# Window attention and two expert layers on one core: the places of the weights in SBUF, and of the identity

## The chip, the cores and the metric

The kernel runs on one core of one Trainium2 chip, in one launch. The metric is device time in microseconds (us), from the run's own clock; the trace comes from a further execution with the hardware profiler on. Engines are called by their short names in the rows: PE is TensorE (PEld its weight loads), DVE VectorE, ACT ScalarE, POOL GpSimd, and SP the engine that issues the DMAs.

## The reference

Three stages follow each other, all in float32. B = 2, H = 8, S = 768, D = 64.

```python
# 1. attention over a window of +-15 keys and the maxima of 24 blocks of 32 keys
k_sum = k.reshape(B, H, nb, block, D).max(axis=3)
v_sum = v.reshape(B, H, nb, block, D).mean(axis=3)
scores_l = scale * q @ k.T            # masked to |i - j| < 16
scores_s = scale * q @ k_sum.T + log(32)
a = softmax(concat([scores_l, scores_s]))
x = a @ concat([v, v_sum])            # -> (1536, 512)
# 2. first layer, 512 -> 2048 -> 512
h = x @ w_in;  g = max(h, 0) + alpha * min(h, 0);  x = g @ w_out
# 3. second layer, with a rational function of h
h = x @ w_in2
g = (a0 + a1*h + a2*h**2 + a3*h**3) / (1 + |b0|*|h| + |b1|*h**2 + 1e-6)
out = g @ w_out2
```

The weights of both layers reach the kernel as 64-bit words, eight bytes for a number, and the kernel makes its own number pairs of them.

## The kernel before

**Numbers in two parts.** Each operand of the layers' matmuls is split into a high part (`xh`, `gh`, `wih`, `woh`) and a low part (`xl`, `gl`, `wil`, `wol`). A product of two operands is three matmuls: high with high, and high with low both ways. All are in the float32r type, with 128 columns loaded and 512 streamed, or 256 in the first part of the first layer.

**Layers.** The 1536 tokens go in three units of 512, the 2048 hidden columns in 16 steps f of 128. `h_mm` (L186) makes h of one unit and one f with 4 x 3 = 12 matmuls on line L195; `y_mm` (L244) adds g's share to the four output tiles with 12 matmuls on line L258. In h of both layers, and in y of the first layer, a weight is the loaded operand (lhsT) and x or g is streamed. In y of the second layer it is the other way round: g is loaded, and the weight `woh` or `wol` is streamed. From about 150 us on, TensorE does a run of 12 for h, then a run of 12 for y, of a step that is some steps behind, and so on. In the second layer h of the last step comes well before the end, so the last 48 matmuls are y alone.

**Weights.** `w_load` (L143) fetches 1 MB of weight words into one of two raw tiles, from the second byte on, with one DMA from the SP queue. `w_split` (L150) turns it into a high and a low tile in steps: ScalarE makes `top` (L161), VectorE joins it with the raw words to `cv` (L163), ScalarE copies cv rounded into the high tile (L137, a helper's line), and GpSimd subtracts the two for the low tile (L173). There are 16 high and 16 low tiles of 4096 bytes in each partition, and they are filled twice, once for each layer. The last ones (`wih7` among them) lie where the attention's buffers lay before, and wait for those to be done with.

**Attention.** It is worked in 24 slices of 64 queries, until about 150 us, with the first layer's first steps between them. TensorE makes scores s (L392), the probabilities p are turned by a transpose against the 128 x 128 identity `ident` (L448), and multiplied with the values (L462). GpSimd multiplies p by the reciprocal of its sum (L442). The order of all this is written out by hand in tables (`ORDERS`, `ENG` and others), which the change leaves as they are.

**Places.** Every tile lies at one byte offset in all 128 partitions. Pools are laid one behind the other from the left (constants, x, g, temporaries, raw, cv, weights), and some, the attention's among them, from the right. SBUF is filled to the end: the last weight tile ends 128 bytes before it. The table gives the offset of some tiles as a remainder modulo 128, as the built program has them.

| tiles | before | after |
|---|---|---|
| `xh`, `xl`, `gh`, `gl`, and the temporaries | 64 | 64 |
| raw, two tiles in turn | 64 and 96 | 64 and 64 |
| `cv` | 0 | 64 |
| all weight tiles | 0 | 64 |
| `ident` | 0 | 64 |
| `qz`, `kc`, `vt`, `p`, `pT` of the attention | 64 | 64 |

The matmuls read offsets of whole multiples of 128 bytes within x, g and weight tiles, so the remainders hold for each matmul's operands.

Of the kernel before, what the change touches and what calls it, by code (L numbers as in the profile page):

```python
# [9 lines left out]
F32 = mybir.dt.float32  # L10
# [3 lines left out]
I16 = mybir.dt.int16  # L14
# [7 lines left out]
P = 128  # L22
# [48 lines left out]
def kernel(  # L71
# [14 lines left out]
    nc = tc.nc  # L86
# [14 lines left out]
    const = ctx.enter_context(tc.tile_pool(name="const", bufs=1))  # L101
# [3 lines left out]
    rawp = ctx.enter_context(tc.tile_pool(name="rawp", bufs=2))  # L105
# [5 lines left out]

    nc.scalar.preload_act_table_set("natural_log_exp_and_others")

    ident = const.tile([P, P], F32, name="ident")
    make_identity(nc, ident)
    al = const.tile([P, NF], F32, name="al")
    na = const.tile([P, 4], F32, name="na")
    ab = const.tile([P, 2], F32, name="ab")
# [22 lines left out]
            e.tensor_scalar(out=out, in0=in_, scalar1=scale, scalar2=None, op0=ALU.mult)  # L141

    def w_load(layer, nm, j):  # L143
        raw = rawp.tile([P, 4100], I16, tag="raw", name="raw")
        words = src_of[layer, nm][:, 2 * j:2 * j + 2, :].rearrange("p a b -> p (a b)").bitcast(I16)
        nc.sync.dma_start(out=raw[:, 1:4097], in_=words)
        raws[layer, nm, j] = raw
        loaded[layer, nm, j] = now[0]

    def w_split(layer, nm, j):  # L150

        raw = raws.pop((layer, nm, j))
        rest = raw.bitcast(I32)[:, 1:2049:2]
        w = cvp.tile([P, 1024], F32, tag="cv", name="cv")
        w3 = w.rearrange("p (a b) -> p a b", a=2)  # L160
        nc.scalar.activation(out=top.bitcast(F16)[:, 1::2], in_=raw.bitcast(BF16)[:, 4:4100:4], func=AF.Copy)  # L161
        yield "low"
        nc.vector.scalar_tensor_tensor(out=w.bitcast(I32), in0=rest, scalar=13, in1=top,  # L163
                                       op0=ALU.logical_shift_right, op1=ALU.bitwise_or)
        if loads:
            w_load(*loads.pop(0))
        yield "hi"
        hi = places[nm, j].tile([P, 2, 512], F32R, tag=f"{nm}h{j}", name=f"{nm}h{j}")
        lo = places[nm, j].tile([P, 2, 512], F32R, tag=f"{nm}l{j}", name=f"{nm}l{j}")
        copy("hi", hi, w3)  # L170
        for i, place in enumerate(("mid", "end")):
            yield place
            eng(place).tensor_tensor(out=lo[:, i, :], in0=w3[:, i, :], in1=hi[:, i, :].bitcast(F32), op=ALU.subtract)  # L173
        wts[layer, nm, j] = (hi, lo)
# [114 lines left out]
    a1 = att_p.enter_context(tc.tile_pool(name="a1", bufs=1, side="right"))  # L289
# [8 lines left out]
    att_e = ExitStack()  # L298
    e1 = att_e.enter_context(tc.tile_pool(name="e1", bufs=1, side="right"))

    NQZ, NVC, NVT = 3, 4, 4
    vlate = []
    HALF = S // 2 + 2 * WINDOW
# [262 lines left out]
    with tc.manual_schedule():  # L566
# [7 lines left out]
        for t in range(-1, LAST + 1):  # L574
# [33 lines left out]
            if t in WLOAD_AT:  # L608
                w_load(*loads.pop(0))
# [110 lines left out]
```

## Time and profile before

| | |
|---|---|
| time, median of 3 runs | 634.09 us (633.48 to 634.31) |
| the profiled execution | 632.7 us, of which the span 630.6 us |
| TensorE busy | 607.3 us, 96% of the span |
| ScalarE, GpSimd, VectorE busy | 384.3, 353.8 and 339.9 us |
| TensorE's share of the chain that ended last | 87% |
| first layer without attention | about 150 to 369 us |
| second layer | about 369 us to the end |

The span is the time from the first to the last instruction in the trace; what the profiled execution took beyond it lies before and after. Matmuls are pipelined: the recorded length of one (around 395 ns for 512 columns) is longer than the time to the next one's start, so the pace of TensorE is read from the runs in the chain of waits, where 12 matmuls of one line stand as one piece with the time that they took together.

### The profile page before, as it was taken

Reading aid. Unit: us, or ns where it says so; the run is one execution under the profiler, and the core shown is the slowest. Engines: PE = TensorE matmul, PEld = TensorE weight load, DVE = VectorE, ACT = ScalarE, POOL = GpSimd, SP = SyncE. Lnnn points to the kernel's source line nnn. Section 1 sums busy time; section 2 is a strip of 40 time slices with the busy share of each in tenths; the row PEclk is TensorE's granted clock in tenths of the full one; section 3 lists DMA queues with packets and bytes.
Section 4 is the critical chain, followed back from the end, with each engine's and each line's share of the span. In section 5 each row is a group of like instructions: output and inputs, shape, how many; then the busy total and the mean of one; then the engine's idle time right before and its main releaser. Section 6 shows DMA issues by size and latency. Waiting matters only on the chain.

```text
span 630.6 us, 8589 instructions
## 1 busy us (share of the span) xinstructions
PE 607.3 (96%) x3192; PEld 496.0 (79%) x3192; DVE 339.9 (54%) x494; ACT 384.3 (61%) x665; POOL 353.8 (56%) x343
## 2 busy tenths in 40 slices
PE   5689999999999999999999999999999999999997
PEld 2467989987888888888888888888888888888885
DVE  4756677753221111045555277776566666566664
ACT  1779798877343333367777457776466666466663
POOL 3266779666512222237667457886366666466662
PEclk9869999999999999999999999999999999999999
DMA  8997476525100000025545101000000000100001
GB/s 294 314 312 266 161 239 221 190 80 200 68 1 1 1 0 1 0 75 192 188 172 183 58 1 67 1 0 2 36 32 1 0 1 1 68 0 2 0 2 67
DMA packets 17129, 55.09 MB, mean 87 GB/s; under 512 B 2368, under 2 KB 4416, under 8 KB 12992
## 3 DMA queue, kind: packets, MB, share of 16 engines
q1 hardware_dynamic: 17088, 54.55, 25.0%
q8 instruction: 25, 0.41, 0.3%
q14 instruction: 16, 0.13, 0.1%
HBM read 51.39 MB, written 3.15 MB: 86 GB/s over the span
## 4 chain that ended last, share of the span: by engine, by line
PE 87%; ACT 4%; DMA 3%; DVE 2%; POOL 2%; issue 1%; SPq 1%; ACTq 0%; DVEq 0%
PE y L258 41%; PE h L195 41%; PE s L392 1%; PE pt L448 1%; PE po L462 1%; DMA raw<-in_w_in 1%; PE vps L357 1%; DMA na<-in_pa 1%; ACT top L161 1%; DMA kt<-in_kT 1%; POOL p L413 1%; ACT p L422 1%; DVE cv L163 1%; SPq L336 0%; ACT pT L137 0%
## 5 line engine op out<-in xcount | busy, mean ns | idle before, releaser
L195 PE MATMUL h<-xh,wih 128*128 128x512 f32 (+1 forms) x416 | 158.0, 380 | 0.0
L195 PE MATMUL h<-xl,wih 128*128 128x512 f32 (+1 forms) x416 | 157.3, 378 | 0.1
L195 PE MATMUL h<-xh,wil 128*128 128x512 f32 (+1 forms) x416 | 157.1, 378 | 0.0
L242 POOL TENSOR_TENSOR gl<-tp,gh 128x512 fp32r<-128x512 f32 (+1 forms) x75 | 94.3, 1258 | 85.8 <-ACT gh L137 84.4
L137 ACT ACTIVATE gh<-tp 128x512 fp32r<-128x512 f32 (+1 forms) x76 | 46.2, 608 | 94.6 <-PE y L258 50.7
L195 PEld LDWEIGHTS h<-xl,wih 128*128 128x128 f32 x416 | 78.4, 188 | 16.5 <-issue 0.5
L195 PEld LDWEIGHTS h<-xh,wih 128*128 128x128 f32 x416 | 78.4, 189 | 16.4 <-ACT pT L137 0.5
L195 PEld LDWEIGHTS h<-xh,wil 128*128 128x128 f32 x416 | 78.3, 188 | 16.0
L258 PE MATMUL y<-gh,woh 128*128 128x512 f32 (+1 forms) x224 | 82.9, 370 | 0.0
L258 PE MATMUL y<-gl,woh 128*128 128x512 f32 (+1 forms) x224 | 81.2, 362 | 0.0
L258 PE MATMUL y<-gh,wol 128*128 128x512 f32 (+1 forms) x224 | 81.2, 362 | 0.0
L163 DVE SCALAR_TENSOR_TENSOR cv<-raw,top 128x1024 int32<-128x1024 int32 x32 | 59.8, 1870 | 30.5 <-ACT top L161 23.1
L258 PE MATMUL y<-woh,gh 128*128 128x512 f32 x192 | 75.9, 395 | 0.0
L258 PE MATMUL y<-wol,gh 128*128 128x512 f32 x192 | 75.8, 395 | 0.0
L258 PE MATMUL y<-woh,gl 128*128 128x512 f32 x192 | 75.3, 393 | 0.0
L228 DVE SCALAR_TENSOR_TENSOR tu<-tu,h 128x512 f32<-128x512 f32 x48 | 33.0, 687 | 71.4 <-ACT h L227 62.8
L217 POOL TENSOR_SCALAR tu<-tv,ab 128x512 f32<-128x512 f32 x48 | 37.3, 777 | 61.0 <-ACT tv L215 61.0
L218 POOL TENSOR_TENSOR tu<-tu,tv 128x512 f32<-128x512 f32 x48 | 62.4, 1299 | 4.0
L242 POOL TENSOR_TENSOR gl<-tu,gh 128x512 fp32r<-128x512 f32 (+1 forms) x28 | 32.4, 1157 | 52.6 <-ACT gh L137 52.6
L208 DVE SCALAR_TENSOR_TENSOR tp<-h,tp 128x512 f32<-128x512 f32 (+1 forms) x28 | 17.2, 614 | 72.2 <-ACT tp L137 72.2
L226 ACT ACTIVATE h<-tu,lnb 128x512 f32<-128x512 f32 x48 | 33.2, 691 | 31.3 <-DVE tp L220 28.9
L208 DVE SCALAR_TENSOR_TENSOR tu<-h,tu 128x512 f32<-128x512 f32 (+1 forms) x28 | 17.2, 613 | 64.7 <-ACT tu L137 64.7
(79 smaller groups left out, 1063.3 us busy)
## 6 DMA issues: line engine op xcount, KB each, us to landing
raw<-in_w_in SPq DMA_DIRECT2D x16, 1024.0 KB, 4.6
raw<-in_w_out SPq DMA_DIRECT2D x16, 1024.0 KB, 4.6
qz<-in_qT SPq DMA_DIRECT2D x25, 256.0 KB, 5.1
vc<-in_vS SPq DMA_DIRECT2D x24, 192.0 KB, 5.1
kt<-in_kT SPq DMA_DIRECT2D x16, 208.0 KB, 5.2
vt<-in_vS SPq DMA_DIRECT2D x12, 256.0 KB, 4.9
out<-stage SPq DMA_DIRECT2D x12, 256.0 KB, 2.1
al<-in_alpha SPq DMA_DIRECT2D x1, 8.0 KB, 6.5
```

The lines of the kernel that those rows point to most:

```text
L137: e.activation(out=out, in_=in_, func=AF.Copy, scale=1.0 if scale is None else scale)
L161: nc.scalar.activation(out=top.bitcast(F16)[:, 1::2], in_=raw.bitcast(BF16)[:, 4:4100:4], func=AF.Copy)
L163: nc.vector.scalar_tensor_tensor(out=w.bitcast(I32), in0=rest, scalar=13, in1=top, op0=ALU.logical_shift_right, op1=ALU.bitwise_or)
L195: nc.tensor.matmul(out=ps, lhsT=a, rhs=b, start=(c == 0 and m == 0), stop=(c == NC - 1 and m == 2))
L208: nc.vector.scalar_tensor_tensor(out=t, in0=ps, scalar=0.0, in1=t, op0=ALU.max, op1=ALU.subtract)
L217: nc.gpsimd.tensor_scalar(out=q, in0=v, scalar1=ab[:, 1:2], scalar2=ab[:, 0:1], op0=ALU.mult, op1=ALU.add)
L218: nc.gpsimd.tensor_tensor(out=q, in0=q, in1=v, op=ALU.mult)
L226: nc.scalar.activation(out=A, in_=q, func=AF.Ln, scale=2.0 ** -LN_SHIFT, bias=lnb)
L228: nc.vector.scalar_tensor_tensor(out=q, in0=q, scalar=one, in1=A, op0=ALU.add, op1=ALU.mult)
L242: (eng("gl") if (u, f) != steps[-1] else nc.vector).tensor_tensor(out=gl, in0=t, in1=gh.bitcast(F32), op=ALU.subtract)
L258: nc.tensor.matmul(out=yps[c][:, c0:c0 + n] if layer == 0 else yps[c], lhsT=a, rhs=b, start=(f == 0 and c0 == 0 and m == 0), stop=(f == NF ...
L357: nc.tensor.matmul(out=vmean[b][0:KEYS, :], lhsT=mean[:, z0:z0 + KEYS], rhs=vt[b, i], start=(i == 0), stop=(i == NV - 1))
```

## The change

The raw tile is made 4160 16-bit words wide where it had 4100, that is 8320 bytes for 8200. The DMA, the conversion and the words that they touch are the same. Two raw tiles of 8200 bytes, each rounded up to 32, end at a multiple of 128, and so everything behind them started there; two of 8320 end 64 bytes past one. To make room, the identity leaves the pool of constants on the left, where it took 512 bytes, and is made in the attention's pool on the right, which is given up after the attention.

```diff
-    ident = const.tile([P, P], F32, name="ident")
-    make_identity(nc, ident)
     al = const.tile([P, NF], F32, name="al")
...
     def w_load(layer, nm, j):
-        raw = rawp.tile([P, 4100], I16, tag="raw", name="raw")
+        raw = rawp.tile([P, 4160], I16, tag="raw", name="raw")
...
     e1 = att_e.enter_context(tc.tile_pool(name="e1", bufs=1, side="right"))
 
+    ident = a1.tile([P, P], F32, name="ident")
+    make_identity(nc, ident)
     NQZ, NVC, NVT = 3, 4, 4
```

The instructions of TensorE, VectorE, ScalarE and SP stand in the same order as before. Lines between L114 and L299 are two lower after the change. On GpSimd, at the start of the program, the identity's memset stood ahead of two small ones (`lnb` and `exb` are constants of the second layer, `bias` is the attention's mask):

```order
L716 UNCONDITIONAL_BRANCH
masks.py:197 MEMSET ident 128x128
L121 MEMSET lnb 128x1
L122 MEMSET exb 128x1
L309 MEMSET bias_130 128x120
masks.py:199 ISA
masks.py:199 AFFINE_SELECT ident<-ident 128x128
```

After the change, the same stretch of GpSimd's program reads:

```order
L716 UNCONDITIONAL_BRANCH
L119 MEMSET lnb 128x1
L120 MEMSET exb 128x1
masks.py:197 MEMSET ident 128x128
L309 MEMSET bias_130 128x120
masks.py:199 ISA
masks.py:199 AFFINE_SELECT ident<-ident 128x128
```

The memset went behind the two small ones, and the select that completes the identity kept its place.

The other difference is one wait. On ScalarE, near the end of the attention, the copy into the high tile `wih7` waited for VectorE's cv alone (semaphores in brackets, `top`, `tp` and `gh` belong to the conversion and to the first layer):

```order
L161 ACTIVATE top_95<-raw_1727 128x1024 [waits DMAHW5_49]
L204 ACTIVATE tp_1944<-h_1931 128x512 [waits PE_49]
L137 ACTIVATE wih7_2039<-cv_1913 128x1024 [waits DVE_49]
L137 ACTIVATE tp_1944<-tp_1944,al_88 128x512 [waits Activation_49]
L137 ACTIVATE gh_1947<-tu_1883 128x512 [waits Pool_49]
```

After the change, the same five instructions are:

```order
L159 ACTIVATE top_90<-raw_1727 128x1024 [waits DMAHW5_49]
L202 ACTIVATE tp_1944<-h_1931 128x512 [waits PE_49]
L135 ACTIVATE wih7_2039<-cv_1913 128x1024 [waits DVE_49,Pool_49]
L135 ACTIVATE tp_1944<-tp_1944,al_83 128x512 [waits Activation_49]
L135 ACTIVATE gh_1947<-tu_1883 128x512 [waits Pool_49]
```

The order is the same; `wih7` lies 320 bytes further left and now touches a second buffer of p, so its copy also waits for GpSimd's last product there (L442), for which the low tile `wil7` had waited before.

## Rows read from the trace of the kernel before

**Rows 1.** Page, busy us (share of the span) and instructions of each engine

```profile
PE 607.3 (96%) x3192; PEld 496.0 (79%) x3192; DVE 339.9 (54%) x494; ACT 384.3 (61%) x665; POOL 353.8 (56%) x343
```

**Rows 2.** Page, the chain that ended last: shares of the span by line

```profile
PE y L258 41%; PE h L195 41%; PE s L392 1%; PE pt L448 1%; PE po L462 1%; DMA raw<-in_w_in 1%; PE vps L357 1%; DMA na<-in_pa 1%; ACT top L161 1%; DMA kt<-in_kT 1%; POOL p L413 1%; ACT p L422 1%; DVE cv L163 1%; SPq L336 0%; ACT pT L137 0%
```

**Rows 3.** Chain in order of time: start us, us, what

```profile
201.67 2.80 PE y L258 x12
204.47 2.80 PE h L195 x12
...
442.19 2.79 PE y L258 x12
444.99 2.80 PE h L195 x12
447.79 2.76 PE y L258 x12
...
615.19 11.02 PE y L258 x48
```

**Rows 4.** Stretches: us, busy (x) of PE, PEld, DVE, ACT, POOL, clock, DMA share, GB/s

```profile
150.00:369.00 219.00, 219.00 (x940) 176.48 (x939) 70.34 (x72) 113.06 (x162) 96.45 (x75) 1.00 0.21 76
...
200.00:240.00 40.00, 40.00 (x173) 32.22 (x172) 4.84 (x7) 13.65 (x23) 9.87 (x8) 1.00 0.00 0
320.00:360.00 40.00, 40.00 (x173) 32.20 (x173) 16.95 (x13) 23.48 (x32) 26.39 (x21) 1.00 0.40 147
```

**Rows 5.** Identity: GpSimd's timeline (start us, us), and its readers (ns min/median/max, first start)

```profile
0.74 0.20 POOL masks.py:197 MEMSET ident<- 128x128 f32 x1 [0.29 <-POOLq L708]
...
1.18 0.29 POOL masks.py:199 TENSOR_SCALAR_AFFINE_SELECT ident<-ident 128x128 f32<-128x128 f32 x1
...
L448 PE MATMUL pt<-ident,p x96: 272/273/469, 17.7 to 141.8; 128*120 128x128 f32 x96
```

**Rows 6.** Timeline of GpSimd and ScalarE around the copy into wih7

```profile
138.29 1.00 POOL L442 TENSOR_TENSOR p<-p,d 128x480 f32<-128x480 f32 x1
139.23 1.30 POOL L242 TENSOR_TENSOR gl<-tu,gh 128x512 fp32r<-128x512 f32 x1
...
148.20 1.05 ACT L137 ACTIVATE wih<-cv 128x1024 fp32r<-128x1024 f32 x1
```

**Rows 7.** Raw and cv: instructions on them (ns min/median/max), two conversions in turn

```profile
L161 ACT ACTIVATE top<-raw x32: 1349/1380/1401, 24.1 to 412.0; 128x1024 f16<-128x1024 bf16 x32
L163 DVE SCALAR_TENSOR_TENSOR cv<-raw,top x32: 1216/1906/2346, 28.1 to 414.5; 128x1024 int32<-128x1024 int32 x32
...
L173 POOL TENSOR_TENSOR wil<-cv,wih x32: 1273/1295/1306, 34.6 to 388.8; 128x512 fp32r<-128x512 f32 x32
...
287.16 2.34 DVE L163 SCALAR_TENSOR_TENSOR cv<-raw,top 128x1024 int32<-128x1024 int32 x1 [1.54 <-ACT top L161]
...
292.75 2.35 DVE L163 SCALAR_TENSOR_TENSOR cv<-raw,top 128x1024 int32<-128x1024 int32 x1 [1.60 <-ACT top L161]
```

**Rows 8.** Single matmuls at the end of two h runs, 447.4 and 441.8 us (busy, mean ns)

```profile
L195 PE MATMUL h<-xl,wih 128*128 128x512 f32 x1 | 0.4, 398 | 0.0
L195 PE MATMUL h<-xh,wil 128*128 128x512 f32 x1 | 0.4, 392 | 0.0
...
L195 PE MATMUL h<-xh,wil 128*128 128x512 f32 x1 | 0.4, 397 | 0.0
L195 PE MATMUL h<-xl,wih 128*128 128x512 f32 x1 | 0.4, 394 | 0.0
```

**Rows 9.** Chain in order of time, runs of 256 columns in the first layer

```profile
106.38 1.42 PE y L258 x12
107.80 1.41 PE h L195 x12
...
112.69 1.36 PE h L195 x12
```

**Rows 10.** Two matmuls that follow each other in a first-layer h run, 205.3 us

```profile
L195 PE MATMUL h<-xh,wih 128*128 128x512 f32 x1 | 0.4, 393 | 0.0
```

## Prediction

> **What bounds the kernel now.** I read the page's busy times first. TensorE is busy for 96% of the span [rows 1], and from 150 us, where the attention ends, it never pauses: 219.00 of 219.00 us up to the second layer [rows 4]. The shares of the chain of waits say the same: two lines of TensorE, L195 (h) and L258 (y), are 41% of the span each [rows 2]. So next to nothing on another engine is worth a microsecond after 150 us. What counts there is how fast TensorE gets through one matmul after another.
>
> The chain in order of time gives that rate, since h and y stand in it as runs of 12 matmuls [rows 3]. A run of 512-column matmuls lasts 2.80 us in the first layer, for h and for y: 2.80 / 12 = 233.3 ns from one matmul to the next. The granted clock of that stretch is 1.00, the upper level of 2.4 GHz [rows 4], where 512 columns alone need 512 / 2.4 = 213.3 ns. So about 20 ns of each matmul are not its columns. Are they other engines' doing? Two stretches of 40 us, one with VectorE, ScalarE and GpSimd busy for 5, 14 and 10 us and no DMA, one with 17, 23 and 26 us and a DMA share of 0.40, hold 173 matmul records each [rows 4]. So the 20 ns belong to TensorE and its own operands.
>
> One thing in the chain does move that rate. In the second layer h still takes 2.80 us a run, but y alternates between 2.76 and 2.79 us, and the closing 48 matmuls of y, with no h between them, last 11.02 us, or 229.6 ns each [rows 3]. What differs in y there is the operands' roles. Everywhere else a weight (0 past a multiple of 128) is loaded and x or g (64 past) streams; there g is loaded and the weight streams. The change touches just these places, and gives both operands 64.
>
> **The change part by part.** *Identity.* Its memset, 0.20 us at 0.74 us, goes behind two that write one column each; the select that finishes it stays where it was, at 1.18 us, and the first transpose is at 17.7 us [rows 5]. Cost nothing: 16 us of cover. Were the cover gone, it would be the 0.2 us of the memset. As the streamed operand of 96 transposes it goes from 0 to 64; a transpose is recorded at 273 ns [rows 5], and if its pace moved by the 1.5% that y's does, 96 times 4 ns make 0.4 us, either way. I take 0.
>
> *The new wait.* ScalarE's copy into wih7 now waits for GpSimd's product on p. That product is over at 138.29 + 1.00 = 139.29 us, the copy starts at 148.20 us [rows 6]: 8.9 us of cover. If it were late, the product with alpha and the gh copy queue behind it on ScalarE, and y on TensorE waits for gh. I take 0.
>
> *Places under the other engines.* The conversion has its raw tile at 64 and at 96 by turns now, and writes cv at 0. ScalarE's part lasts 1349 to 1401 ns over all 32 [rows 7], so the two places differ by at most 0.05 us. VectorE's ranges from 1216 to 2346 ns, but two that follow each other, and so read different raw tiles, last 2.34 and 2.35 us; GpSimd's subtractions that read cv have a median of 1295 ns [rows 7], and one that reads tu and gh, all at 64, lasts 1.30 us at 139.23 us [rows 6]: no dearer. 32 conversions times 0.05 us are 1.6 us, of which only those on the chain before 150 us count: top is 1% of it and cv 1% [rows 2]. Bounds plus and minus 0.2 us; I take 0. The transfers keep their shapes and their start two bytes into the tile. The trace has no separate row for raw tiles at 96 and at 64; loads are 1% of the chain, some 6 us [rows 2], and if half of them, those into the second tile, moved by a tenth, it would be 0.3 us, either way. I take 0.
>
> *Operands of the matmuls.* This is the term that decides. 88 runs of h and 40 of y in the first layer are 512 columns wide, all with places 0 and 64; 48 runs of y in the second have the roles swapped; another 32 runs are 256 wide. No row shows 64 with 64 in a steady run. It stands only at the seams of the second layer, where the last h of a run streams x while the first g is loaded: one such matmul is recorded at 392 ns where its neighbour has 398, another at 397 beside 394 [rows 8]. One below, one above: undecided. So I bound it. From below: no stall at all, 213.3 ns or 2.56 us a run, saves 0.24 x 128 + 0.215 x 48 = 41 us. From above: the 256-wide runs show that the very same instructions at the same places take 1.36 or 1.41 to 1.42 us [rows 9], some 4%, according to how loads and streams fall together; 4% on 176 runs of 2.80 us is 20 us more. The rows nearest to the new state are y's of the second layer, where the loaded operand already lies at 64: (2.76 + 2.79) / 2 = 2.775 us. I take it for all 512-wide runs: 128 x 0.025 = 3.2 us saved, y of the second layer unchanged, the 256-wide runs 0, as they lie among waits on ScalarE and VectorE.
>
> The Trainium skill speaks against even this. "TensorE: Matmul & The Clock Gate", section "Step-by-step: what each phase is for", says that the loading of weights and the moving operand have read ports of their own and that a load takes nothing from the running matmul; by it, and with the 2.5 ns of its section "Back-to-back issue gap" as an estimate, a matmul would take 216 ns wherever its operands lie. The trace does not agree in size: 233.3 ns, and y's 229.6 at other places.
>
> *Sum.* The profiled execution took 632.7 us, with a span of 630.6 us and 2.1 us around it. 632.7 - 3.2 = 629.5 us. It lies 1.4 us under the median of the runs shown, 634.09, so for a median I add it back: 630.9 us.
>
> **The rivals.**
> *A large gain (chance 0.10).* Equal places bring loads and streams into the better of the two states of the 256-wide runs. 2.80 x 1.36 / 1.42 = 2.68 us: 0.12 x 128 + 0.095 x 48 = 19.9 us, so 614 us. For it: that state exists, and it lasts through whole runs [rows 9]. Against it: no 512-wide run of the first layer ever shows it, while 256-wide ones at one set of places show both.
>
> *Places don't matter (0.20).* y's 2.76 and 2.79 are then an effect of order, since the weight streams there in the sequence high, low, high. The time stays at 634.1 us. For it: even and odd runs of y differ by more (0.03 us) than the even ones differ from 2.80 [rows 3], though all have the same places modulo 128. The rule of the Trainium skill on separate ports, cited above from "TensorE: Matmul & The Clock Gate", would have it so as well.
>
> *The streamed operand's own place counts (0.10).* Weights stream well from 0 and lose that at 64, loaded operands don't matter. Then y of the second layer goes to 2.80 us: 44 x 0.025 + (4 x 2.80 - 11.02) = 1.1 + 0.2 = 1.3 us more, 635.4 us. For it: it explains why only this y is quicker. It sits on the line between no change and slower.
>
> *Equal places collide (0.18).* A load and a stream whose starts agree modulo 128 get in each other's way more often than two whose starts differ, and every matmul goes to the slower of the two recorded lengths that now alternate, 398 instead of the mean of 393 and 398 [rows 8, 10]. That is 2.5 ns x 12 = 0.03 us on each of 128 runs, 3.8 us, and y of the second layer goes with them, from 2.775 to 2.83 us, 2.6 us more: 640.5 us. It decides from the first 512-wide run on. The 397 at the seam speaks for it, the 392 against [rows 8].
>
> **How the numbers follow.** Forecast 0.42 (630.9 us), large gain 0.10, no change 0.20, streamed place 0.10, collision 0.18. A measurement of this kernel can tell about 0.2%, 1.27 us, from no change. Faster by more: 0.42 + 0.10 = 0.52. Within: 0.20 and four tenths of the streamed-place case, 0.24. Slower: the rest of that and the collision, 0.24. The range reaches down to 616 us, near the large gain, whose size is the least known of all, and up to 638.5 us, which takes in the streamed place with its small terms and a collision of about two thirds the size; outside lie about half of the one and half of the other rival. For the likeliest case alone it is 628 to 632.5 us, a mean run of 2.75 to 2.79 us.
>
> **What would show it right or wrong.** In the chain of the changed kernel, h and first-layer y should stand at about 2.775 us a run where 2.80 stood, with y of the second layer as it was; 2.68 would be the large gain, 2.80 with y at 2.80 the streamed place, 2.83 and more the collision, and the old numbers no influence. The matmul records in two 40 us stretches would go from 173 to 174 or 175. The identity is right if the first transpose still starts at about 17.7 us, the new wait if the wih7 copy starts within a few tenths of 148.2 us. I am wrong altogether if the time moves while the run lengths stay.

## The result and the profile after

The changed kernel takes 622.78 us (621.42 to 623.92, 4 runs) where the kernel before, on the same chip, takes 633.79 us (633.09 to 634.31): a ratio of 0.9826, with a 95% interval of 0.9803 to 0.9849. It is 11.0 us faster; 3.2 us were forecast. The two profiled executions, from which the rows are read, took 632.7 and 623.16 us and differ by 9.5 us.

The chain of the changed kernel in order of time, start us and us, at the places of [rows 3]. Lines between L114 and L299 are two lower now, so h is L193 and y is L256:

```profile
201.80 2.72 PE y L256 x12
204.52 2.72 PE h L193 x12
...
441.16 2.72 PE y L256 x12
443.88 2.72 PE h L193 x12
```

Once the attention is over, every run of 512 columns is 2.72 us, h and y, first layer and second, odd and even, up to the last steps: 226.7 ns a matmul for 233.3. The alternation of 2.76 and 2.79 is gone.

The runs of 256 columns in the attention, where [rows 9] had 1.42, 1.41 and 1.36:

```profile
107.84 1.44 PE y L256 x12
109.28 1.44 PE h L193 x12
...
112.80 1.43 PE y L256 x12
114.23 1.44 PE h L193 x12
...
129.10 2.75 PE h L193 x12
```

They are slower, and both states have become one. The first 512-wide runs, four of them between pieces of the attention, last 2.75 to 2.76 us and not yet 2.72. The first of h starts at 129.10 us; before, it stood in the same chain at 127.29 us. This start moves by more than that from one profiled execution to the next, as the later runs show, so only 0.02 to 0.08 us for each of 32 runs is surely the places' doing, 0.04 us on average.

Near the end a wait has appeared that the kernel before did not have. These are the last pieces of the chain:

```profile
612.09 0.76 DVE tp L228
...
612.93 0.64 ACT gh L135
...
613.61 3.07 PE y L256 x12
```

and this is its row among TensorE's waits (total us, times, longest us):

```profile
PE y L256 <- ACT gh L135: 1.1, 1, 1.1
```

The stretches with little and with much work on other engines, answering to [rows 4] (columns as there):

```profile
150.00:369.00 219.00, 219.00 (x967) 181.38 (x968) 73.75 (x77) 117.28 (x168) 102.21 (x78) 1.00 0.22 77
200.00:240.00 40.00, 40.00 (x178) 33.11 (x178) 5.54 (x8) 13.93 (x23) 10.28 (x8) 1.00 0.00 0
320.00:360.00 40.00, 40.00 (x178) 33.15 (x177) 17.33 (x17) 24.14 (x32) 26.67 (x21) 1.00 0.38 132
```

173 matmul records became 178 in both, at the same granted clock.

**The sum of it.** In the two profiled executions the span fell from 630.6 to 621.0 us. 88 runs of h and 40 of y in the first layer give 128 x 0.08 = 10.2 us. y of the second layer gives 44 x 2.775 + 11.02 - 48 x 2.72 = 2.6 us. The wait and the slower first matmuls behind it take back 3.07 + 1.1 - 2.72 = 1.4 us, and the later start of the 512-wide runs 1.8 us: 10.2 + 2.6 - 1.4 - 1.8 = 9.6 us.

### The profile page after: what moved, and what is told of

Its sections match the earlier page's. It is cut to its first block, busy times and chain, and to the rows that moved or that the text cites. A ratio compares the mean times of both kernels' runs of the same rounds, so it can differ in the third digit from the quotient of the medians.

```text
span 621.0 us, 8590 instructions
## 1 busy us (share of the span) xinstructions
PE 596.2 (96%) x3192; PEld 497.3 (80%) x3192; DVE 338.9 (55%) x494; ACT 383.7 (62%) x665; POOL 354.6 (57%) x343
## 4 chain that ended last, share of the span: by engine, by line
PE 75%; DVE 10%; ACT 6%; DMA 5%; POOL 2%; issue 1%; SPq 1%; DVEq 0%; ACTq 0%
PE h L193 35%; PE y L256 35%; DVE tp L228 2%; DVE tp L218 2%; DVE h L227 2%; DVE tu L226 2%; PE s L392 2%; ACT h L224 2%; ACT h L225 2%; DMA kt<-in_kT 1%; DVE tp L217 1%; PE po L462 1%; DMA raw<-in_w_in 1%; PE pt L448 1%; PE vps L357 1%
## 5 line engine op out<-in xcount | busy, mean ns | idle before, releaser
L193 PE MATMUL h<-xh,wih 128*128 128x512 f32 (+1 forms) x416 | 156.3, 376 | 0.0
L193 PE MATMUL h<-xl,wih 128*128 128x512 f32 (+1 forms) x416 | 155.3, 373 | 0.0
L193 PE MATMUL h<-xh,wil 128*128 128x512 f32 (+1 forms) x416 | 155.1, 373 | 0.0
L193 PEld LDWEIGHTS h<-xl,wih 128*128 128x128 f32 x416 | 78.5, 189 | 14.3 <-issue 0.5
L193 PEld LDWEIGHTS h<-xh,wih 128*128 128x128 f32 x416 | 78.6, 189 | 14.0 <-ACT pT L135 0.5
L193 PEld LDWEIGHTS h<-xh,wil 128*128 128x128 f32 x416 | 78.5, 189 | 13.8
L256 PE MATMUL y<-gh,woh 128*128 128x512 f32 (+1 forms) x224 | 81.9, 366 | 0.0
L256 PE MATMUL y<-gh,wol 128*128 128x512 f32 (+1 forms) x224 | 80.4, 359 | 0.0
L256 PE MATMUL y<-gl,woh 128*128 128x512 f32 (+1 forms) x224 | 80.3, 359 | 0.0
L256 PE MATMUL y<-woh,gh 128*128 128x512 f32 x192 | 74.8, 390 | 1.1 <-ACT gh L135 1.1
L256 PE MATMUL y<-wol,gh 128*128 128x512 f32 x192 | 74.7, 389 | 0.0
L256 PE MATMUL y<-woh,gl 128*128 128x512 f32 x192 | 74.5, 389 | 0.0
```

The costliest lines, as they stand in the source:

```text
L193: nc.tensor.matmul(out=ps, lhsT=a, rhs=b, start=(c == 0 and m == 0), stop=(c == NC - 1 and m == 2))
L256: nc.tensor.matmul(out=yps[c][:, c0:c0 + n] if layer == 0 else yps[c], lhsT=a, rhs=b, start=(f == 0 and c0 == 0 and m == 0), stop=(f == NF ...
```

## The experiments

**Which places?** Three kernels set x and g on one hand, and the weights on the other, to other bytes; a fourth makes only the identity's half of the change. `ident` is in the attention's pool in e2 and e4. The expectations go by theories. A: the pace hangs on whether the places of the loaded and the streamed operand agree modulo 128. B: the place of one operand alone counts (B1, the weights at 64; B2, x and g at 64, and the weights at 64 too). D, which came up with the matmuls alone (below) and before e4: the two places have to agree modulo 256.

```diff
# e1_w64: 64 unused bytes between raw and cv; e2_both0: the same, and 64 ahead of x; e3_x0_w64: 64 ahead of x alone
+    padp = ctx.enter_context(tc.tile_pool(name="padp", bufs=1))
+    pad = padp.tile([P, 16], F32, name="pad")
+    nc.gpsimd.memset(pad, 0.0)
     cvp = ctx.enter_context(tc.tile_pool(name="cvp", bufs=2))
...
# e4_ident_only: the change without
-        raw = rawp.tile([P, 4100], I16, tag="raw", name="raw")
+        raw = rawp.tile([P, 4160], I16, tag="raw", name="raw")
```

> The kernel before with 64 unused bytes put between raw and cv: the weights and cv lie at 64 as after the change, the raw tiles stay at 64 and 96 and the identity stays among the constants. If the weights' place is the whole of the change (theories A and B): runs of 12 at 2.72 us and 621.5 to 624 us. If the raw tile's or the identity's place, or the smaller waits behind them, gave a part: between that and 634 us by that part; if they gave all of it, 634 us and 2.80 us.

> x, g and the temporaries at 0 and the weights at 0 modulo 128 (the identity in the attention's pool, 64 bytes unused ahead of x and 64 behind raw, raw at 0 and 32). Theory A (places that agree): 2.72 us a run, 621.5 to 624.5 us. Theory B1 (weights run well at 64 whatever x does): 2.80 us, 633 to 635 us. Theory B2 (x and g at 64 are well placed and weights at 64 too): slower than before, over 634 us.

> The mixed pair the other way round: x, g and the temporaries at 0, the weights at 64 (64 unused bytes ahead of x, the rest as before the change). Theory A: 2.80 us for runs that stream x or g, y of the second layer 2.76 to 2.80 us, 633 to 635 us. Theory B1 (weights at 64 are what counts): 2.72 us, 621.5 to 624.5 us. If the streamed operand's place counts, x at 0 would be quicker than 2.80 us and y of the second layer, which streams weights from 64, slower than 2.76.

> The identity's half of the change alone: it lies with the attention, the raw tile has its old width, so x and g lie 512 bytes further left (64 modulo 256) and the weights 512 too (128 modulo 256). Theory D and the prediction's step on the identity: as before, 2.80 us a run, within 0.2% of 633.8 us. If the identity's place carries part of the 11 us: below 632.5 us with the runs at 2.80.

| kernel | x, g and weights modulo 128 | loaded minus streamed place, modulo 256 | us | ratio to before (95%) |
|---|---|---|---|---|
| before | 64, 0 | 64 | 633.79 | |
| after | 64, 64 | 0 | 622.78 | 0.9826 (0.9803 to 0.9849) |
| e1_w64 | 64, 64 | 128 | 634.64 | 1.0016 (0.9993 to 1.0039) |
| e2_both0 | 0, 0 | 128 | 632.03 | 0.9976 (0.9961 to 0.9991) |
| e3_x0_w64 | 0, 64 | 64 | 633.30 | 0.9993 (0.9983 to 1.0003) |
| e4_ident_only | 64, 0 | 64 | 633.50 | 1.0003 (0.9989 to 1.0017) |

(The third column holds for h, and for y of the first layer; in y of the second the roles and so the sign are swapped. A ratio is always to the kernel before on the same chip, whose median was 633.74 us beside e1 to e3, 633.32 beside e4, f1 and f2, and 632.55 beside f3 and f4.)

e1 decides: x, g and the weights lie 64 past a multiple of 128 there, as after the change, and nothing is won. So theory A, agreement modulo 128, is wrong, and so is B1. In e4 the identity's place is worth nothing that the interval could tell, about 0.2%. A run of y and a run of h in e1, from its chain:

```profile
203.30 2.80 PE y L261 x12
206.10 2.80 PE h L198 x12
```

e2 was not foreseen by any of the theories. It is quicker than the kernel before by 1.7 us, clear of its interval, with runs of 2.78 and 2.79 us in both layers:

```profile
203.01 2.79 PE y L262 x12
```

Its difference of 128 is that of e1, whose runs stand at 2.80. Why the two are not alike is open.

**The matmuls alone.** The kernel m1 sent along with them holds nothing but matmuls. Its blocks look like this, with the places in the name of the output (n columns, m streamed, s loaded, in bytes from the start of each operand's tile). Both tiles start 128 past a multiple of 256 in the built program, so the differences are as the names say, and the remainders 128 more. The kernel reads the 64-bit weight words as if they were float32, so the numbers multiplied are not the weights; its paces are those of the whole kernel all the same.

```diff
+        for r in range(36):
+            nc.tensor.matmul(out=bank("n512m64s0e", r)[:, :512], lhsT=B[:, 0 + 128 * (r % 4):0 + 128 * (r % 4) + 128], rhs=A[:, 16:16 + 512], start=True, stop=True)
```

> A kernel of matmuls alone (float32r, 128 columns loaded for each, real numbers), in blocks of 36 that differ only in the byte places of the loaded and the streamed operand; the three stages of the reference are left out. What is read is the pace in each block. Theory A (the pace hangs on whether the two places agree modulo 128): 226.7 ns for 512 columns at 0/0 and 64/64, 233 ns at 64/0 and 0/64, and 226.7 again where the loaded operand lies 128, 256, 512 or more bytes on. Theory B (the place of one operand alone counts): 0/0 like one of the mixed pairs, 64/64 like the other. Theory C (the pace was won by the order or by the neighbours in the kernel, not by places): the same pace in all blocks. For 256 columns, 120 ns where the places agree and 113 to 118 ns where they differ, by A.

Its chain, start us and us of each block of 36:

```profile
17.96 8.20 PE n512m0s0e L39 x36
26.15 8.26 PE n512m64s0e L41 x36
34.41 8.39 PE n512m0s64e L43 x36
42.81 8.18 PE n512m64s64e L45 x36
...
101.35 8.40 PE n512m0s128e L59 x36
109.75 8.24 PE n512m0s192e L61 x36
118.00 8.17 PE n512m0s256e L63 x36
126.17 8.40 PE n512m0s320e L65 x36
134.57 8.19 PE n512m0s512e L67 x36
...
192.37 4.32 PE n256m0s0e L81 x36
196.69 4.24 PE n256m64s0e L83 x36
200.93 4.09 PE n256m0s64e L85 x36
205.02 4.30 PE n256m64s64e L87 x36
```

The granted clock is 1.00 in all these blocks. 8.17 to 8.20 us, or 227 to 228 ns, at a difference of 0, 256 and 512; 8.39 to 8.40, or 233 ns, at 64, 128 and 320; 8.24 to 8.26, or 229 ns, at 192, which is what 0 less 64 is modulo 256. The other differences tried here, 16 to 112 and 0 less 16, 32 and 96, took 8.34 to 8.43. So the period is 256 bytes, and 128 is as bad as 64. 0 with 0 and 64 with 64 are alike, and the mixed pairs slower, so no operand's place decides alone, and theory B is out. That tells e1 from the changed kernel: 64 and 64 modulo 128 are 64 and 192 modulo 256 in e1, and 64 and 64 in the changed one. It also goes with y of the second layer before the change, whose difference is 192: its closing 48 matmuls, 11.02 us, are 229.6 ns each, and in e3, with 192 at other remainders, y has the same 2.76 and 2.79 us and the same 11.02. With 256 columns agreement costs: 4.30 and 4.32 against 4.09 and 4.24 us. Theory C is out: VectorE and GpSimd are not busy at all in these blocks, nor is ScalarE.

**The rule at the kernel's size.** f1 puts x, g and the weights all at multiples of 256, f4 the weights at 0 with x and g at 64.

```diff
# f1_agree256_at0: as e2_both0, but 192 unused bytes at either place; f4_diff192: 128 behind raw alone
+    pad = padp.tile([P, 48], F32, name="pad")
```

> x, g and the weights all at a multiple of 256 (192 unused bytes ahead of x and 192 behind raw, raw at 0 and 32, cv at 0, the identity with the attention). Theory D (agreement modulo 256, whatever the remainder): 2.72 us a run, 621.5 to 624 us, as after the change. Theory F (64 past a multiple of 128, as the change says, or the raw tiles at 64 and 64): 2.79 to 2.80 us, 632 to 635 us.

> The fourth difference at the size of the kernel: x and g at 64 and the weights at 0 modulo 256 (128 unused bytes behind raw, the old raw width, the identity with the attention). Loaded minus streamed place is 192 where x or g streams, and 64 in y of the second layer. By the matmuls alone (theory D): 228.8 ns or 2.745 us a run for h and y of the first layer, 2.80 us for y of the second; 128 x 0.055 us less and 48 x 0.025 us more, so about 628 us, 0.991 of before. If the weights' remainder modulo 128 decided (here 0, as before the change): 633.5 us and 2.80 us.

f1 takes 622.45 us (ratio 0.9829, 0.9809 to 0.9848), the same as the changed kernel within either interval, with 2.72 us a run:

```profile
445.86 2.72 PE y L262 x12
```

So remainders of 0 and of 64 modulo 256 do equally well, and the raw tiles' places are of no account: theory F is out. f4 takes 628.61 us (0.9932, 0.9910 to 0.9955) where about 628 was expected. In its first layer the runs are as expected, in the second h does only half as well:

```profile
201.67 2.75 PE y L259 x12
204.42 2.75 PE h L196 x12
...
441.82 2.76 PE h L196 x12
444.59 2.80 PE y L259 x12
447.39 2.79 PE h L196 x12
```

The same instructions at the same difference take 2.75 us in the first layer, where y has the difference 192 too, and 2.76 and 2.79 us in turn in the second, between runs of y at 2.80. So at 192 the neighbours count: alternation came only between runs of the slower kind, as with y's odd and even runs in [rows 3]. Why odd and even differ was not tested; they also read different halves of a weight tile and use their buffers in turn.

**What is left of the pace.** A second kernel of matmuls alone asks what the remainder does and whether the load's size counts.

```diff
+        for r in range(36):
+            nc.tensor.matmul(out=bank("n512m0s128c64e", r)[0:64, :512], lhsT=B[:, 32 + 128 * (r % 4):32 + 128 * (r % 4) + 64], rhs=A[:, 0:0 + 512], start=True, stop=True)
```

> A second kernel of matmuls alone, as the first (the reference's stages are left out), to settle what the first showed: 226.7 ns where loaded and streamed place agree modulo 256, 228.8 ns at a difference of 192, 233 ns at 64 and 128. Theory D (the difference modulo 256 alone counts): 226.7 ns at 16/16, 32/32, 128/128 and 192/192; near 226.7 or up to 233 ns at differences of 4, 8, 248 and 252; 230 to 234 ns at 144, 176 and 208. Theory E (an operand's own place counts too): the four agreeing pairs differ from 226.7. If what is left over the 213.3 ns of the columns comes from the load's own reads, loading 64 columns instead of 128 halves it at places that agree (220 ns), and 32 columns leave a quarter (217 ns); if it is a fixed cost of each matmul, 226.7 ns stay. 256 columns: 120 ns at 0, 113.3 at 64, 117.8 at 192; the rest unknown.

Blocks of 36 from its chain (c is the number of columns loaded):

```profile
67.93 8.16 PE n512m0s252c128e L51 x36
76.09 8.31 PE n512m16s16c128e L53 x36
84.41 8.18 PE n512m32s32c128e L55 x36
92.59 8.21 PE n512m128s128c128e L57 x36
...
117.57 4.24 PE n256m0s64c128e L65 x36
...
130.31 4.32 PE n256m0s160c128e L71 x36
...
143.10 8.28 PE n512m0s0c96e L77 x36
...
159.61 8.16 PE n512m0s128c96e L81 x36
167.77 8.28 PE n512m0s0c64e L83 x36
...
192.69 8.33 PE n512m0s0c32e L89 x36
```

Agreeing pairs named 32 and 128 are at 227 to 228 ns, so theory D holds there; at 16 and 16 the pace is 231 ns, so an operand's own place counts at 16 bytes off a multiple of 32, and theory E is right in that. The sole block off agreement that reaches the best pace with 128 columns loaded is a loaded place 4 bytes short of it (8.16). Loading 64 or 32 columns does not bring the pace towards 213 ns: 8.28 and 8.33 us are 230 and 231 ns. So what is left over the 213.3 ns is not the loads' reads counted one by one, as I had thought possible. And with fewer columns loaded agreement is no longer the best place: with 96 loaded, a difference of 128 takes 8.16 us and agreement 8.28. With 256 columns streamed, 0 and 64 took 4.09 us in the first kernel and take 4.24 here, behind another block: two states again, though what chooses was not tested. A difference of 160 takes 4.32 there, as much as agreement.

**The closing wait.** f2 and f3 change the order of the last step in the changed kernel, and the changed kernel ran once more beside f3.

```diff
# f2_last_h_early
+            if held:
+                u, f = held.pop()
...
+                if len(h_list) == 1:
+                    held.append(h_list.pop(0))
+                    h_mm(*held[0])
# f3_last_p_first: f2 and
-            for fn, u_f in sorted(late.pop(s, ()), key=lambda x: order.index(x[0])):
+            for fn, u_f in sorted(late.pop(s, ()), key=lambda x: 0.5 if x == (act2_p, steps[-1]) else order.index(x[0])):
```

> The changed kernel with the last h run of the second layer issued one y run earlier, so that 60 matmuls of y instead of 48 lie behind it. After the change TensorE waits 1.1 us near 612 us for the last gh (1.4 us with what follows), which it did not before. If that wait is the faster pace running into the fixed length of the last step's elementwise chain: the wait goes, and the time falls by 1.1 to 1.4 us to 621 to 622 us, ratio to before about 0.980. If the wait comes from elsewhere (the closing of y or the output): no change, 622.8 us.

> The changed kernel with the last h run issued one y run early (as in the run before) and, for the last step alone, VectorE's and ScalarE's first polynomial part put ahead of the step before's quotient, where VectorE waits for ScalarE's logarithm and exponential. If the closing wait is the length of VectorE's and ScalarE's steps one after another (5.17 us a step): the last gh is there up to 1.4 us earlier and the time is 0.5 to 1.4 us under the changed kernel. If only what lies behind the last h counts: no change against it.

> The changed kernel once more, beside the two others and the kernel before on one chip: 0.980 to 0.985 of before, 2.72 us a run in every 512-wide stretch, and the wait for the last gh near 612 us again if it belongs to the program and not to one execution.

f2 took 622.92 us (0.9838, 0.9819 to 0.9857): no gain. The last h was there earlier, and the wait stayed, with a second one on gl:

```profile
PE y L256 <- ACT gh L135: 1.2, 1, 1.2
...
PE y L256 <- POOL gl L240: 0.3, 1, 0.3
```

f2 moved more than the last h: y's runs came later with it, and ScalarE's copy into gh stood idle for 2.81 us until y gave the buffer up.

```profile
602.87 0.63 ACT L135 ACTIVATE gh<-tp 128x512 fp32r<-128x512 f32 x1 [2.81 <-PE y L256]
```

So f2 alone doesn't say whether the distance from the last h counts. The chain of the changed kernel says what sets the wait there: from 538 us to the last gh no piece of it is TensorE's. VectorE's and ScalarE's steps hang on one another for a whole step, and tp (L217) comes around each 5.17 us.

```profile
602.50 0.61 DVE tp L217
...
603.13 0.76 DVE tp L218
...
607.67 0.61 DVE tp L217
```

While h and y alternate, TensorE needs 2 x 2.72 = 5.44 us for a step and this loop keeps up. Once h is done a step is a single y of 2.72 us, and TensorE catches up with the loop. f1, with runs of 2.72 us, has the same wait (`PE y L262 <- ACT gh L141: 1.1, 1, 1.1`); f4, with 2.75 to 2.80, has none on gh. No run here made the loop shorter, so this part rests on the chain and on these two. f3, which tried to shorten it for the last step, took 625.44 us (0.9885, 0.9861 to 0.9908) and is slower than the changed kernel, which took 623.10 us on the same chip (0.9847, 0.9820 to 0.9875; its wait for the last gh is 1.1 us again). TensorE stood still longer in f3, and then ran at the lower level of the clock for a while. Stretches of f3 (columns as in [rows 4]):

```profile
606.00:612.00 6.00, 3.80 (x16) 2.54 (x15) 3.76 (x7) 2.51 (x4) 1.96 (x2) 1.00 0.00 0
612.00:616.00 4.00, 4.00 (x12) 3.10 (x11) 1.94 (x3) 0.63 (x1) 0.00 (x0) 0.57 0.00 0
```

TensorE was busy for 3.80 of 6 us, and in the 4 us behind the mean granted clock is 0.57, for most of that stretch 1.2 and not 2.4 GHz. In the changed kernel, where it stood still once for 1.1 us, the clock stays at 1.00 from 606 to 616 us. None of the versions tried beats the changed kernel by more than the intervals hold.

## Why the prediction was right, and where it was not

**What bounds the kernel: right.** The whole gain is in the pace of the 512-wide matmuls, and it is the same whatever the other engines do. That next to nothing on another engine is worth a microsecond after 150 us held up to the last step, where the closing wait took 1.4 us.

**Identity, new wait, raw and cv: right, though two signs were badly chosen.** e4 puts the identity's place at 1.0003. The first transpose starts at 18.5 us and not at 17.7, and the copy into wih7 is 1.6 us later than before, not within a few tenths: such starts moved by about 2 us between two executions of the changed kernel (18.5 and 20.3, 149.81 and 151.78), so they tell nothing. What tells is the cover. The copy into wih7 starts at 149.81 us and GpSimd's product on p is over at 140.08 + 0.98 = 141.06 us, so the cover of [rows 6] is still 8.75 us:

```profile
140.08 0.98 POOL L442 TENSOR_TENSOR p<-p,d 128x480 f32<-128x480 f32 x1
...
149.81 1.05 ACT L135 ACTIVATE wih<-cv 128x1024 fp32r<-128x1024 f32 x1
```

f1, with raw at 0 and 32, runs as the changed kernel with raw at 64 and 64.

**Operands of the matmuls: the direction right by luck, the term mis-sized.** The step that failed is "the rows nearest to the new state are y's of the second layer": 2.775 us was taken for all runs, 2.72 was measured, so 128 x 0.025 = 3.2 us stood for 10.2, and "y of the second layer unchanged" for 2.6 us more. The reason lies in how the places were sorted. Modulo 128, the old pairs were 0 and 64, and y of the second layer looked half-way to 64 and 64. Modulo 256, as the matmuls alone show, old h had a difference of 64, old y of the second layer one of 192, and the new pairs 0: y's runs were a third kind and no step towards the new one. So the reason for a gain did not hold, and that there was one, and that the result lies in the range, is luck: 622.78 us is about as far from the forecast of 630.9 as from the large gain's 614, and the range was wide enough to reach from one to the other. The seams of [rows 8] were real pairs of 64 and 64 modulo 256, but a single matmul between others, in a pace on which its neighbours count, could not show it.

**The 256-wide runs, taken at 0: not quite.** They lost some 0.04 us each, about 1.3 us; at agreement they have the slower pace alone.

**The rivals.** The large gain was wrong in its mechanism: the quick state of the 256-wide runs is not the one that came, and those runs left it. "Places don't matter" fell with the matmuls alone, and so did the rule beside it: the Trainium skill ("TensorE: Matmul & The Clock Gate", section "Step-by-step: what each phase is for") has loads and streams on read ports of their own, so that a load takes nothing from the running matmul, and the trace does not agree for float32r, where moving the loaded operand by 64 bytes takes the matmul from 227 to 233 ns. Whether the ports are the reason no run here shows. "The streamed operand's own place counts" fell with e3, where the weights stream from 64 and y of the second layer keeps its 2.76 and 2.79 us. "Equal places collide" fell too, for 512 columns; with 256, agreement is among the slowest places. The point that decides, modulo 256, was in none of them: the change's own words, 64 bytes past a multiple of 128, describe e1 as well, which gains nothing.

**The closing wait** was not foreseen. A faster TensorE ran into a loop of 5.17 us a step on the other engines, and gave 1.4 us back.

## What to carry to other kernels

Where float32r matmuls with 128 columns loaded and 512 streamed fill TensorE, compare the byte places of the loaded and the streamed operand modulo 256, and make them equal at a multiple of 32: it was 3% of TensorE's pace here, for a few bytes of padding. With 256 columns streamed, or 96 loaded, agreement was not the best place here, so other shapes want their own blocks. Before explaining a pace by a remainder, try the remainder of twice and half the size in blocks of matmuls alone; one run of 240 us held 29 blocks. When TensorE gets faster, compare its new step with the length of the loop on the other engines, here 5.44 and 5.17 us, and look at the end, where one of the two runs of a step falls away.

## What was not expected of the hardware

- The pace of float32r matmuls hangs on the difference of the places with a period of 256 bytes: 227 ns at 0, 233 at 64 and 128, 229 at 192 (128 columns loaded, 512 streamed, granted clock 1.00). With 512 columns no pair was below 226.7 ns, against 213.3 for the columns. Why 256, and what the 13 ns left are, stays open; loads of fewer columns did not shorten them.
- Off agreement the pace can have two states at the same places, and each lasts for a run or a block: 2.76 and 2.79 us a run at 192, 4.09 and 4.24 us a block of 256 columns at 64. What runs beside it counts; what chooses was not isolated. At agreement only one was seen, but for the 2.75 us of the first runs between the attention's work.
- With 256 columns agreement is the slow place: 119 to 120 ns there (4.30 to 4.32 us / 36), 113.6 to 120 ns off it, with 160 as slow as agreement. With 384 columns, differences of 0 and 192 are alike (6.27 and 6.24 us for 36), 64 and 128 a little slower (6.36 and 6.34).
